# A convolution and feed-forward kernel: step 1's blocks cross the partition halves on ScalarE instead of by SyncE's transfers

## The chip, the cores and the metric

The kernel runs on one core of one Trainium2 chip. The metric is the device time of one launch in microseconds: 2280.98 us as the median of three timed runs (2280.73 to 2281.51). One more run was taken with the hardware profiler; all rows shown are from it. TensorE (PE) multiplies, VectorE (DVE), ScalarE (ACT) and GpSimd (POOL) compute elementwise, SyncE (SP) issues transfers, and POOL issues transfers too. All transfers are carried out by the same 16 DMA engines.

## The reference

A causal convolution of width 7 along the sequence, with one softmax-normalized filter for each of 8 heads, followed by a feed-forward block with a quick GELU:

```python
batch, seq, d_model = (8, 4096, 192)      # kernel_size 7, n_heads 8
w = np.exp(w - max); w = w / (sum + 1e-09)
out = np.einsum('hk,bskhg->bshg', w, x_unf)          # the convolution
h = x @ w_in                                         # [32768, 192] @ [192, 2048]
g = h * (1.0 / (1.0 + np.exp(-1.702 * h)))
return (g @ w_out).astype(np.float32)                # [32768, 2048] @ [2048, 192]
```

The weights arrive as 64-bit floats and are turned into 32-bit ones on the chip.

## The kernel before

The 32768 tokens are worked off in 32 steps ("big" 0 to 31) of two batches with 512 tokens each. A step has two products. The first one (line 614) multiplies the convolved input by w_in, the second one (line 989, in step 0 lines 820 and 825) multiplies the activated result by w_out. From step 1 on both are written in a Strassen-like form with fewer multiplications: sums of input blocks, of weight blocks ("forms") and of result blocks take the place of some matmuls. The schedule is written out by hand; each engine works through its own instructions in program order.

The tile `conv_t` has 3 planes of 13 blocks, each 128 partitions by 256 columns. `own(big)` is plane 0 for even steps and plane 2 for odd ones; plane 1 is shared. The convolution writes six blocks (C11 to C32) into the step's own plane, and `sums_c` adds seven or eight more (V1 to V8). The product works on pairs of partition halves, so every block is also needed with its halves exchanged: upper 64 partitions to the lower 64 and the other way round, in plane 1. `cross(big, b0, b1)` makes that copy with two transfers on SyncE's queue (line 541).

- `prepare(big)` lists the convolution's VectorE work, the sums and the crossings. In step 1 the sums run on VectorE, in later steps on POOL (line 393 and 391). Its first crossing is that of V1 alone, which opens the step: `fetch` multiplies with it first. Then blocks C11 to C22 cross, and at the end of the list all others.
- `cross_when` holds a crossing back until the plane is free; for step 1 the two larger ones are therefore issued together, in the middle of step 0's second product, where `need("all 1")` stands. In later steps the crossings are cut into pieces of three blocks (`pieces`), spread over the second product.
- Step 0's second product is `second_first`. While it runs, `add_forms` makes the forms: copies on ScalarE (line 435 and 433) and additions done by accumulating transfers which POOL issues (line 437). ScalarE also copies partial results there: `act.copy(to, dst)` (line 827), c12 and c21 from bank `a` (lines 864 and 873), and the sums of line 885.
- In the same stretch the taps of step 2's convolution begin: `tap` multiplies on ScalarE (line 516). The taps of one third are then added up by accumulating transfers, issued by POOL in `end_taps` (line 530), and those of another third by POOL itself (line 518). V1 of step 2 needs both.
- `end_forms` (line 441) turns the signs of four forms on ScalarE during step 1's first product, `hidden`, after their accumulating transfers have landed. ScalarE's copies of line 651, activations of lines 636 and 640 and VectorE's sums of line 655 belong to `hidden` too. In step 1, the transposes of the next input (line 473, `turn_next`) and one sum (`EARLY_G_1`) stand in the second half of `hidden` on VectorE; in later steps the transposes stand in the first half, and that sum is an accumulating transfer.

The order on POOL's queue in this stretch is: accumulations of the forms (line 437), three accumulations of taps (g<-g, line 530), one more into `conv_t`, the last four accumulations of the forms, two more of taps, then the six adds of line 518 and the sums of line 393 and 391, the first of which is V1 of step 2.

Of the kernel before, what the change touches and what calls it, by code (L numbers as in the profile page):

```python
# [15 lines left out]
def kernel(  # L16
# [29 lines left out]
    nc = tc.nc  # L46
# [34 lines left out]
    vec, act = nc.vector, nc.scalar  # L81
    halves = [slice(0, R), slice(R, P)]
# [75 lines left out]
    conv_t = consts.tile([P, 3, NB, T], F32)  # L158
# [17 lines left out]
    def own(big):  # L176
        return conv_t[:, big % 2 * 2, :, :]
# [135 lines left out]
    for c in range(NC):  # L313
        part = sel[:, c, :].rearrange("i (h q) -> i h q", h=2)
        for sign in (1, -1):
            nc.gpsimd.affine_select(
                out=part,
                in_=part,
# [219 lines left out]

    def cross(big, b0, b1):
        for o in range(2):  # L540
            nc.sync.dma_start(
                out=conv_t[halves[1 - o], 1, b0:b1, :], in_=own(big)[halves[o], b0:b1, :]
            )

    def copy_over(b):

# [9 lines left out]
    def cross_now(early, big, b0, b1):  # L556
        if early or big == 1:
            cross(big, b0, b1)
        else:
            pieces.extend((big, b, min(b + 3, b1)) for b in range(b0, b1, 3))  # L560

    def cross_piece():
        if pieces:
            cross(*pieces.pop(0))
# [729 lines left out]
```

## Time and profile before

| | us |
|---|---|
| median of three timed runs | 2280.98 |
| lowest, highest | 2280.73, 2281.51 |
| profiled execution, its own time | 2281.64 |
| its span, first to last instruction | 2279.60 |
| DVE busy in the span | 1942.0 |
| ACT busy | 1563.4 |
| POOL busy | 849.1 |

How to read the rows: in a timeline row stand the start in us, the duration in us, the engine, the source line, the operation, the names written and read, shapes and how many instructions were merged; in brackets the idle time of the engine before it and what ended it. In a row of stretches stand from:to, the length, then for each engine its busy time and its number of instructions, then the granted TensorE clock as a share of full speed, the share of the DMA engines and GB/s; where only one line is asked for, PE and PEld (weight loads) alone stand there. In the chain of waits: start, duration, what. In the DMA view: the queue's packets, MB and share of the 16 engines, or an issue's names, count, KB each and the median us from issue to landing. In groups by line: count, busy us, mean ns of one, idle time before.

### The profile page before, as it was taken

Reading aid. Unit: us, or ns where it says so; the run is one execution under the profiler, and the core shown is the slowest. Engines: PE = TensorE matmul, PEld = TensorE weight load, DVE = VectorE, ACT = ScalarE, POOL = GpSimd, SP = SyncE. Lnnn points to the kernel's source line nnn. Section 1 sums busy time; section 2 is a strip of 40 time slices with the busy share of each in tenths; the row PEclk is TensorE's granted clock in tenths of the full one; section 3 lists DMA queues with packets and bytes.
Section 4 is the critical chain, followed back from the end, with each engine's and each line's share of the span. In section 5 each row is a group of like instructions: output and inputs, shape, how many; then the busy total and the mean of one; then the engine's idle time right before and its main releaser. Section 6 shows DMA issues by size and latency. Waiting matters only on the chain.

```text
span 2279.6 us, 60958 instructions
## 1 busy us (share of the span) xinstructions
PE 2268.2 (100%) x25214; PEld 1198.7 (53%) x25214; DVE 1942.0 (85%) x2794; ACT 1563.4 (69%) x2968; POOL 849.1 (37%) x834
## 2 busy tenths in 40 slices
PE   9999999999999999999999999999999999999999
PEld 5445555555555555555555555555555555555556
DVE  8888888888888888888888888888888888888877
ACT  8657766677766677666776666776667766667754
POOL 1544442344432444424444233443244442344400
PEclk9999999999999999999999999999999999999999
DMA  9976566665567565666656666556756566674443
GB/s 205 161 147 136 117 118 126 130 136 114 113 126 144 121 132 113 128 127 126 139 114 117 126 134 132 121 111 125 142 120 135 114 127 128 124 142 83 91 99 70
DMA packets 270227, 285.76 MB, mean 125 GB/s; under 512 B 118016, under 2 KB 206080, under 8 KB 269824
## 3 DMA queue, kind: packets, MB, share of 16 engines
q0 software_dynamic: 57648, 150.69, 36.8%
q1 hardware_dynamic: 210656, 130.80, 25.5%
q8 instruction: 198, 3.24, 0.6%
q14 instruction: 77, 0.63, 0.1%
q10 hardware_dynamic: 1648, 0.39, 0.1%
HBM read 53.15 MB, written 25.17 MB: 34 GB/s over the span
## 4 chain that ended last, share of the span: by engine, by line
PE 98%; DMA 1%; ACT 0%; DVE 0%; POOL 0%; issue 0%; SPq 0%; DVEq 0%; ACTq 0%; POOLq 0%
PE slot L614 35%; PE slot L989 34%; PE sums L614 15%; PE sums L989 12%; PE slot L820 2%; DMA w_out_s<-w_form 1%; DMA xin<-in_x_dram 0%; POOL conv_t L518 0%; ACT conv_t L1094 0%; DVE xt L473 0%; DMA conv_t<-conv_t 0%; DVE conv_t L504 0%; SPq L99 0%; ACT conv_t L357 0%; ACT conv_t L356 0%
## 5 line engine op out<-in xcount | busy, mean ns | idle before, releaser
L614 PE MATMUL slot<-conv_t,w_in_s 64*128 64x512 f32 x3740 | 864.9, 592 | 4.5 <-DMA conv_t<-conv_t 2.6
L989 PE MATMUL slot<-g,w_form 128*32 128x256 f32 x7024 | 710.4, 379 | 0.0
L614 PEld LDWEIGHTS slot<-conv_t,w_in_s 64*128 64x128 f32 x3740 | 373.2, 187 | 435.3 <-issue 356.8
L393 DVE TENSOR_TENSOR g<-g 128x1024 f32<-128x1024 f32 x372 | 449.1, 1235 | 4.5 <-ACT g L640 1.3
L989 PEld LDWEIGHTS slot<-g,w_form 128*32 128x32 f32 x7024 | 372.9, 110 | 120.4
L614 PE MATMUL sums<-conv_t,w_in_s 64*128 64x512 f32 x1660 | 409.4, 591 | 0.3 <-DVE w_in_s L376 0.3
L640 ACT ACTIVATE g<-room 128x1024 f32<-128x1024 f32 x310 | 325.8, 1077 | 72.1 <-DVE room L655 70.2
L1014 ACT COPY room<-slot 32x256 f32<-32x256 f32 x434 | 159.3, 367 | 310.9 <-PE slot L989 309.8
L989 PE MATMUL sums<-g,w_form 128*32 128x256 f32 x2648 | 368.8, 379 | 0.0
L989 PE MATMUL slot<-g,w_out_s 128*32 128x256 f32 x4080 | 318.9, 380 | 0.0
L965 POOL DMA_DIRECT2D g<-g x124 | 106.2, 857 | 496.2 <-PE slot L989 157.7
L614 PEld LDWEIGHTS sums<-conv_t,w_in_s 64*128 64x128 f32 x1660 | 171.4, 187 | 186.9 <-issue 140.8
L518 POOL TENSOR_TENSOR conv_t<-conv_t,g 128x512 f32<-128x512 f32 x180 | 261.6, 1453 | 14.1 <-POOL conv_t L518 2.6
L530 POOL DMA_DIRECT2D g<-g x120 | 104.7, 890 | 421.3 <-PE sums L989 128.7
L651 ACT COPY room<-slot 128x512 f32<-128x512 f32 x434 | 231.5, 601 | 40.3 <-PE slot L614 40.3
L516 ACT ACTIVATE g<-xt,cw 128x512 f32<-128x512 f32 x360 | 248.7, 730 | 2.2
L989 PEld LDWEIGHTS slot<-g,w_out_s 128*32 128x32 f32 x4080 | 164.5, 110 | 132.9 <-ACT g L636 22.7
L636 ACT ACTIVATE g<-slot 128x512 f32<-128x512 f32 x334 | 180.8, 598 | 45.1 <-PE slot L614 24.6
L989 PEld LDWEIGHTS sums<-g,w_form 128*32 128x32 f32 x2648 | 177.8, 110 | 36.8
L504 DVE SCALAR_TENSOR_TENSOR conv_t<-xt,cw,conv_t 128x512 f32<-128x512 f32 (+1 forms) x198 | 190.7, 963 | 4.6
L393 POOL TENSOR_TENSOR conv_t<-conv_t 128x256 f32<-128x256 f32 x180 | 186.8, 1051 | 9.4
L1014 ACT COPY room<-sums 32x256 f32<-32x256 f32 x217 | 79.6, 367 | 144.2 <-PE sums L989 142.5
(204 smaller groups left out, 2903.9 us busy)
## 6 DMA issues: line engine op xcount, KB each, us to landing
g<-g POOLq DMA_DIRECT2D x124, 512.0 KB, 5.7
xin<-in_x_dram SPq DMA_DIRECT2D x240, 180.0 KB, 4.3
conv_t<-conv_t SPq DMA_DIRECT2D x180, 192.0 KB, 3.2
g<-g POOLq DMA_DIRECT2D x120, 256.0 KB, 3.7
out_dram<-osbs SPq DMA_DIRECT2D x186, 128.0 KB, 5.0
g<-room POOLq DMA_DIRECT2D x31, 512.0 KB, 5.5
conv_t<-g POOLq DMA_DIRECT2D x60, 256.0 KB, 4.7
g<-osbs POOLq DMA_DIRECT2D x30, 512.0 KB, 4.7
```

What stands on the lines that cost most here:

```text
L393: eng.tensor_sub(v(dst), v(a), v(b))
L504: vec.scalar_tensor_tensor(out=dst, in0=src, scalar=tap, in1=dst, op0=ALU.mult, op1=ALU.add)
L516: act.mul(home, conv_src(big, c, k), cw[:, c, k : k + 1])
L518: nc.gpsimd.tensor_add(dst, dst, home)
L530: nc.gpsimd.dma_start(out=out, in_=src, accum_op=ALU.add)
L614: nc.tensor.matmul(slot[h], w_in_s[halves[h], a, v * P : (v + 1) * P], src, start=first, stop=True, skip_group_check=True,)
L636: act.activation(dst[:, :, h, :], src[h].rearrange("p (o t) -> p o t", o=2), AF.Gelu_apprx_sigmoid)
L640: act.activation(dst.rearrange("p o h t -> p h o t"), src.rearrange("p h (o t) -> p h o t", o=2), AF.Gelu_apprx_sigmoid,)
L651: act.copy(bank(dst, h), bank(src, h))
L965: nc.gpsimd.dma_start(out=spot(dst), in_=spot(a), accum_op=ALU.add)
L989: nc.tensor.matmul(dst, w, t, start=first, stop=last, skip_group_check=True)
L1014: act.copy(to, d)
```

## The change

The copies that `cross` makes for step 1 go from SyncE's transfers to copies by ScalarE, except where only one block is copied (V1, the one that opens the step). That is two calls with two halves each: blocks C11 to C22 (64 partitions by 1024) and the eight blocks from C31 on (64 by 2048). All other steps keep their transfers.

```diff
     def cross(big, b0, b1):
         for o in range(2):
-            nc.sync.dma_start(
-                out=conv_t[halves[1 - o], 1, b0:b1, :], in_=own(big)[halves[o], b0:b1, :]
-            )
+            out, src = conv_t[halves[1 - o], 1, b0:b1, :], own(big)[halves[o], b0:b1, :]
+            if big == 1 and b1 - b0 > 1:
+                act.copy(out, src)
+            else:
+                nc.sync.dma_start(out=out, in_=src)
```

On ScalarE the four copies stand, in program order, between the fourth copy of line 827 (room<-slot, 76.60 us in the profile) and the fifth (81.75 us); on SyncE the four transfers stood behind the pair for V1 and ahead of step 0's stores. The order of instructions on PE, VectorE and POOL is the same as before.

## The prediction

> **What bounds the kernel now.** First the head of the profile's page: TensorE (PE) is busy for 2268.2 of 2279.6 us, so any gain has to come out of some 11 us in which PE waits, or out of time in which it runs slowly.
>
> ```profile
> span 2279.6 us, 60958 instructions
> ...
> PE 2268.2 (100%) x25214; PEld 1198.7 (53%) x25214; DVE 1942.0 (85%) x2794; ACT 1563.4 (69%) x2968; POOL 849.1 (37%) x834
> ```
>
> Then the stretches, for the matmuls of line 614 alone: the first product of step 1, beside that of step 3, which has the same 168 matmuls.
>
> ```profile
> 93.11:139.44 46.33, 42.15 (x168) 23.87 (x168) 0.93 0.76 136
> 383.52:419.77 36.25, 36.25 (x168) 16.70 (x168) 1.00 0.57 112
> ```
>
> Step 1 takes 10.1 us more, at a mean granted clock of 0.93. PE's timeline and the stretches with all engines say where:
>
> ```profile
> 117.96 1.18 PE L614 MATMUL slot<-conv_t,w_in_s 64*128 64x512 f32 x3 [1.56 <-ACT room L651]
> 135.03 4.47 PE L614 MATMUL slot<-conv_t,w_in_s 64*128 64x512 f32 x12 [2.61 <-DMA conv_t<-conv_t]
> ```
> ```profile
> 119.20:122.60 3.40, 3.40 (x10) 1.79 (x8) 3.40 (x3) 2.17 (x4) 2.82 (x3) 0.50 1.04 194
> 136.30:139.70 3.40, 3.40 (x12) 1.36 (x12) 0.83 (x2) 0.00 (x0) 3.10 (x4) 0.50 1.12 223
> ```
>
> Two stalls, 1.56 and 2.61 us, and after each 3.4 us at half clock, which cost 1.7 us of work each: 7.6 us. Smaller slips make up the other 2.5.
>
> The rule that speaks against counting the clock: the Trainium skill, TensorE: Matmul & The Clock Gate, section "HAM oscillation — how this bites in real kernels", asks for "no PE-idle gaps >~3.4µs". Both idle times here are shorter, and each is followed by 0.50; I go by the rows, and the rule's own result is a rival below.
>
> Third the chain of waits: what is late before each stall?
>
> ```profile
> 105.10 11.73 DMA w_out_s<-w_form
> ...
> 116.91 0.52 ACT w_form L441
> 117.43 0.48 ACT room L651
> ...
> 131.63 0.74 POOL conv_t L393
> ...
> 132.90 2.00 DMA conv_t<-conv_t
> ```
>
> Stall 1 is ScalarE (ACT), held by an accumulating transfer that POOL issued at 105.1. Stall 2 is step 2's opening block V1, summed on POOL at 131.63 and only then sent across. Both lead to POOL's queue, whose timeline is:
>
> ```profile
> 94.66 1.85 POOL L437 DMA_DIRECT2D w_form<-w_form  x2 [13.07 <-DMA w_form<-w_form]
> 96.20 3.98 POOL L530 DMA_DIRECT2D g<-g  x3
> 102.73 1.19 POOL L530 DMA_DIRECT2D conv_t<-g  x1 [2.55 <-PE slot L614]
> ...
> 108.18 1.20 POOL L530 DMA_DIRECT2D g<-g  x1 [0.69 <-DMA g<-g]
> 119.70 1.19 POOL L530 DMA_DIRECT2D conv_t<-g  x1 [10.32 <-DMA g<-g]
> 120.45 11.10 POOL L518 TENSOR_TENSOR conv_t<-conv_t,g 128x512 f32<-128x512 f32 x6
> ```
>
> POOL stands 13.07 us until 94.66 for one landing, and everything behind it, including the six adds that end in V1, is pushed back. (The 2.55 us put down to PE are more likely the landing of the first g<-g, which this transfer reads.) What are the transfers stuck behind? The DMA view from 79 to 93 us, and the first row of the same view from 63 to 75:
>
> ```profile
> q0 software_dynamic: 930, 1.26, 54.8%
> q1 hardware_dynamic: 310, 1.53, 48.8%
> ...
> w_form<-w_form POOLq DMA_DIRECT2D x2, 192.0 KB, 14.7
> ```
> ```profile
> q0 software_dynamic: 1348, 2.12, 110.7%
> ```
>
> The 16 engines are full. From 79 to 93 POOL's transfers (software queue) share them with SyncE's (hardware queue), and these are the transfers that the change removes.
>
> **The change, part by part.** It removes four transfers, two of 256 KB and two of 512 KB (1.57 MB). Step 1's V1 pair and all later steps stay.
>
> Removed from DMA: 48.8% of 14 us is 6.8 us of all 16 engines. The other way: alone, POOL's queue moved 2.12 MB in 12 us, 0.177 MB/us; its 1.26 MB would take 7.1 us and end near 86 instead of 93. So POOL's 94.66 becomes about 87.7.
>
> The Trainium skill, SBUF — State Buffer, "SBUF: two separate sides", warns of another cause: POOL cannot write its descriptors while VectorE holds the port they share. By that rule the 13 us would stay, which is the "no change" rival; full engines speak against it.
>
> Added to ACT: four copies of 64 partitions, 1024, 1024, 2048 and 2048 wide, between L827 at 76.60 and L827 at 81.75.
>
> ```profile
> 76.60 0.58 ACT L827 COPY room<-slot 32x512 f32<-32x512 f32 x1 [1.17 <-PE slot L825]
> 81.75 0.58 ACT L827 COPY room<-sums 32x512 f32<-32x512 f32 x1 [4.57 <-PE sums L825]
> 83.51 0.56 ACT L873 COPY slot<-slot 96x512 f32<-96x512 f32 x1 [1.18 <-PE slot L820]
> 85.60 0.73 ACT L516 ACTIVATE conv_t<-xt,cw 128x512 f32<-128x512 f32 x1 [1.52 <-DVE xt L473]
> ...
> 91.08 1.95 ACT L516 ACTIVATE g<-xt,cw 128x512 f32<-128x512 f32 x3
> ...
> 110.50 1.06 ACT L640 ACTIVATE g<-room 128x1024 f32<-128x1024 f32 x1 [1.61 <-DMA conv_t<-g]
> ...
> 116.91 0.52 ACT L441 ACTIVATE w_form<-w_form 128x384 f32<-128x384 f32 x1 [1.19 <-DMA w_out_s<-w_form]
> ```
> ```profile
> L548 ACT COPY conv_t<-conv_t 64x256 f32<-64x256 f32 x4 | 1.6, 404 | 0.5 <-DVE conv_t L504 0.4
> L640 ACT ACTIVATE g<-room 128x1024 f32<-128x1024 f32 x5 | 5.3, 1094 | 1.6 <-DMA conv_t<-g 1.6
> ```
> ```profile
> 78.25 1.62 DVE L393 TENSOR_TENSOR conv_t<-conv_t 128x256 f32<-128x256 f32 x4
> ```
> ```profile
> 86.11 0.63 PE L820 MATMUL slot<-osbs,w_out_s 128*32 128x512 f32 x3
> ```
>
> A half-to-half copy of 256 takes 0.40; an activation of 1024 takes 1.09, so each element adds (1.09 - 0.40)/768 = 0.9 ns and a copy of 2048 takes 2.0. Bounds: 1.9 if the fixed part overlaps, 3.2 if it grows as the 256 copy does (8 x 0.40). I take 2.0, nearest to the wide row. The narrow pair runs from 77.2 to 79.4. The wide pair waits for VectorE's last sum, which ends at 79.87, and ends at 83.9. Queued behind are L827 (ends 84.5 instead of 82.3), L873 (85.1 instead of 84.1), then L516 at 85.60, which waited for VectorE anyway. PE needs L873's bank at 86.11. So it costs nothing: 4.57 + 1.18 + 1.52 us of ACT idleness hide it, with 1.0 us to spare; at the upper bound (1.6 and 3.2 us a copy) L873 ends at 87.9 and PE loses 1.8. A gain from the blocks arriving sooner is excluded: PE starts on them at 93.11 without a wait.
>
> What follows on POOL: the three g<-g need ScalarE's taps (L516), the last of which ends at 93.03. With an issue of 1.19 the group ends about 94.2 instead of 100.18, 6 us sooner. conv_t<-g follows its first landing, so it and the issue at 105.10 come 6 to 8 us sooner; with the same 11.73 us of flight w_out_s<-w_form lands by 111, before ACT asks at about 114. ACT recovers the 1.19 before 116.91 and the 1.61 before 110.50, 2.8 together, more than the 1.56 that PE stalled. Stall 1 goes with its clock window: 3.3 us.
>
> For stall 2, the issue at 108.18 waits for the third g<-g. It comes 5 us sooner if flights stay long, and 11 if they shrink towards the 3.7 us of the page's row for the whole run:
>
> ```profile
> g<-g POOLq DMA_DIRECT2D x120, 256.0 KB, 3.7
> ```
>
> I take 9, as the engines are then nearly empty until 97. V1 lands at 134.9 - 9 = 126, and PE, 3.8 us sooner itself (3.3 and about 0.5 of slips), asks at 132.4 - 3.8 = 128.6. Stall 2 goes as well: 2.6 + 1.7 = 4.3 us. At 5 us sooner 1.3 us of it would be left.
>
> What is late next: VectorE at the end of step 1. Its rows of step 1 (first three, with the page's mean) and of step 3:
>
> ```profile
> 120.13 3.15 DVE L393 TENSOR_TENSOR osbs<-g 128x1024 f32<-128x1024 f32 x1
> ...
> 128.98 2.08 DVE L473 STREAM_TRANSPOSE xt<-xin 128x576 f32<-128x576 f32 x3
> ```
> ```profile
> L393 DVE TENSOR_TENSOR g<-g 128x1024 f32<-128x1024 f32 x372 | 449.1, 1235 | 4.5 <-ACT g L640 1.3
> ```
> ```profile
> 415.65 1.28 DVE L655 TENSOR_TENSOR room<-room,slot 128x512 f32<-128x512 f32 x2 [1.54 <-PE slot L614]
> ...
> 419.87 1.28 DVE L655 TENSOR_TENSOR room<-room,slot 128x512 f32<-128x512 f32 x2 [0.60 <-PE slot L614]
> ```
>
> In its second half step 1 has the transposes (2.08) and one add (1.24) that step 3 has elsewhere: 3.3 us against 2.14 us of idleness in step 3. VectorE ends 1.2 us late, and the second product needs it at once. Before, stall 2 covered that. I charge 1.0 (from 0, if PE has some slack, to 3.1, if one L393 again takes 3.15 instead of 1.24 beside POOL's adds).
>
> Sum: 7.6 (stalls and windows) + 1.2 (half of the 2.5 of slips; 0 to 2.5) - 1.0 = 7.8 us. The profiled run took 2281.64 us around its span of 2279.6, 0.66 above the median of the three timed; off both comes the same 7.8, so 2273.8 for that run and **2273.2** as a median.
>
> **The rivals.** (A) Stall 2 stays: only the first part of POOL's chain moves, V1 still waits for flights that collide with out_dram and xin loads. Gain 3.3 + 0.5, 2277.2. For: the flights after 97 us are as loaded as before. (B) VectorE's tail is longer: a stall of 1.6 brings its own 1.7 of half clock, 3.3 instead of 1.0, 2275.5, and up to 3.1 + 1.7, 2277.0. For: the 3.15 row. Against: POOL's adds move ahead of that stretch. (C) No change, 2281.0: POOL waits for descriptors, not for engines. Against: 54.8% and 48.8% fill them. (D) Slower: ACT becomes the bound before 93 us. If copies across halves of this width run at half the rate, the wide pair takes 8 us, ends at 87.9, and L873 at 89.1: PE waits 3.0 and loses 1.7 to the clock, and the taps, 3.5 us later, end at 96.5, where POOL issues today, so nothing is recovered: 2285.7. It begins to decide when a wide copy takes over 2.5 us (79.9 + 5.0 + 1.15 = 86.1). Against: L548 does the same move without such a penalty. (E) The clock windows come by themselves and stay, so the stalls alone go, 4.2 us: 2276.8. Against: nowhere else before the end does a window stand without a stall. That is what the page on the clock gate would give.
>
> **How the numbers follow.** Forecast 0.68, A 0.06, B 0.13, C 0.06, D 0.05, E 0.02. A measurement of this kernel can tell about 0.2%, 4.6 us, from no change, so faster means under 2276.4: forecast and two thirds of B, 0.77. Same: the rest of B, A, C and E, 0.18. Slower: D, 0.05. The range begins at 2270.9 (all 10.1 us recovered) and ends at 2277.2, which takes in B and A and leaves out C and D.
>
> **What would show it.** Right: POOL's L437 starts near 88 instead of 94.66; the 1.56 and 2.61 us of PE idleness and both stretches at 0.50 are gone; the first product of step 1 takes 37 to 39 us; four ACT copies end near 84, and PE starts at 86.1 as before. Wrong: L437 still near 94 (C); PE late at 86.1 (D); a wait on conv_t<-conv_t near 128 (A); a wait on VectorE or a 0.50 stretch at the start of the second product (B).

## The result, and the profile after

The changed kernel takes 2273.79 us as the median of seven runs (2273.21 to 2274.41), against 2280.98 (2280.08 to 2282.35) for the kernel before: a ratio of 0.9968, with a 95% interval of 0.9957 to 0.9980. The forecast was 2273.2 in a range of 2270.9 to 2277.2.

| | before | forecast | after |
|---|---|---|---|
| POOL's L437 behind its long wait starts | 94.66 | near 88 | 86.70 |
| V1 of step 2 has landed | 134.90 | 126 | 125.94 |
| first product of step 1, us | 46.33 | 37 to 39 | 37.43 |
| second product of step 1, us | 33.91 | 34.9 | 34.81 |
| PE's last matmul starts | 2274.20 | | 2266.26 |
| median, us | 2280.98 | 2273.2 | 2273.79 |

(Lines behind the edit have moved by two: L614 is now L616, L655 is L657, L989 is L991. The copies are L543, V1's transfers L545.) The head of the page, after:

```profile
span 2272.6 us, 60950 instructions
...
PE 2263.4 (100%) x25214; PEld 1214.9 (53%) x25214; DVE 1941.0 (85%) x2794; ACT 1568.8 (69%) x2972; POOL 847.0 (37%) x834
```

PE's busy time fell by 4.8 us although it runs the same 25214 matmuls: one at half clock counts as busy for longer (with the traffic put back, below, one of the same line takes 1.19 us at half clock and 0.59 at full). The rest of the gain was idleness. The stretches of step 1's two products, one view for the matmuls of each line; columns are stretch, length, PE and weight loads, clock, DMA share, GB/s:

```profile
93.00:130.43 37.43, 37.43 (x168) 25.22 (x168) 1.00 0.76 137
```
```profile
130.43:165.24 34.81, 34.42 (x624) 30.14 (x624) 1.00 0.84 169
```

The mean clock of the first product went from 0.93 to 1.00, and PE is busy through all of it. The second product is 0.9 us longer than before (33.91), and the view of PE's waits between 80 and 165 us holds one line only:

```profile
PE slot L991 <- DVE room L657: 0.4, 1, 0.4
```

That is the wait on VectorE's tail for which the prediction had charged 1.0; as a wait it is 0.4 of the 0.9 us, and 0.75 went when the tail was made shorter (below). Where the first product's gain comes from is seen on POOL's timeline, next to the rows shown of before:

```profile
86.70 0.86 POOL L437 DMA_DIRECT2D w_form<-w_form  x1 [5.95 <-DMA w_form<-w_form]
87.77 0.86 POOL L437 DMA_DIRECT2D w_form<-w_form  x1 [0.21 <-DVE w_in_s L391]
...
91.98 2.42 POOL L530 DMA_DIRECT2D g<-g  x2 [0.55 <-ACT g L516]
94.69 1.19 POOL L530 DMA_DIRECT2D conv_t<-g  x1 [0.29 <-issue]
...
96.52 2.93 POOL L437 DMA_DIRECT2D w_out_s<-w_form  x2
98.23 2.45 POOL L530 DMA_DIRECT2D g<-g  x1
109.85 1.19 POOL L530 DMA_DIRECT2D conv_t<-g  x1 [9.17 <-DMA g<-g]
110.60 11.98 POOL L518 TENSOR_TENSOR conv_t<-conv_t,g 128x512 f32<-128x512 f32 x6
```

The wait of 13.07 us shrank to 5.95. What stood behind it came sooner by 8.0 us (L437), 9.95 (the g<-g at 98.23 instead of 108.18) and 9.85 (the adds at 110.60 instead of 120.45). At the end of this chain stand V1's two transfers, on SyncE's timeline and in the DMA view from 123 to 125:

```profile
123.43 1.11 SPq L545 DMA_DIRECT2D conv_t<-conv_t  x2
```
```profile
conv_t<-conv_t SPq DMA_DIRECT2D x2, 64.0 KB, 1.9
```

The second is issued at 123.99 and lands at 125.94. The DMA view from 79 to 93 us:

```profile
q0 software_dynamic: 1392, 1.83, 82.2%
...
w_form<-w_form POOLq DMA_DIRECT2D x4, 192.0 KB, 5.2
```

The hardware queue, 48.8% before, is gone from this stretch; POOL's queue moves 1.83 MB instead of 1.26, and the median of its w_form landings is 5.2 us (four of them) instead of 14.7 (two). The price, on ScalarE's timeline:

```profile
76.98 2.09 ACT L543 COPY conv_t<-conv_t 64x1024 f32<-64x1024 f32 x2
79.78 3.83 ACT L543 COPY conv_t<-conv_t 64x2048 f32<-64x2048 f32 x2 [0.70 <-issue]
83.52 0.57 ACT L829 COPY room<-sums 32x512 f32<-32x512 f32 x1
84.11 0.56 ACT L875 COPY slot<-slot 96x512 f32<-96x512 f32 x1
85.42 0.72 ACT L516 ACTIVATE conv_t<-xt,cw 128x512 f32<-128x512 f32 x1 [0.75 <-DVE xt L473]
```

Four copies in 5.9 us, and L516 still finds its data last at 85.42. PE's waits show nothing near 86.

### The profile page after: what moved, and what is told of

It reads as the page before. It is cut to its first block, busy times and chain, and to the rows that moved or that the text cites. A ratio compares the mean times of both kernels' runs of the same rounds, so it can differ in the third digit from the quotient of the medians.

```text
span 2272.6 us, 60950 instructions
## 1 busy us (share of the span) xinstructions
PE 2263.4 (100%) x25214; PEld 1214.9 (53%) x25214; DVE 1941.0 (85%) x2794; ACT 1568.8 (69%) x2972; POOL 847.0 (37%) x834
## 4 chain that ended last, share of the span: by engine, by line
PE 99%; DVE 1%; ACT 0%; DMA 0%; issue 0%; SPq 0%; ACTq 0%; DVEq 0%
PE slot L616 35%; PE slot L991 33%; PE sums L616 16%; PE sums L991 13%; PE slot L822 2%; DMA xin<-in_x_dram 0%; DVE room L657 0%; DVE xt L473 0%; ACT conv_t L1096 0%; DVE conv_t L504 0%; SPq L99 0%; ACT conv_t L357 0%; DVE room L393 0%; ACT conv_t L356 0%; DVE g L391 0%
## 5 line engine op out<-in xcount | busy, mean ns | idle before, releaser
L616 PE MATMUL slot<-conv_t,w_in_s 64*128 64x512 f32 x3740 | 862.5, 591 | 0.3 <-DVE w_in_s L376 0.3
L991 PE MATMUL slot<-g,w_form 128*32 128x256 f32 x7024 | 710.8, 379 | 0.4 <-DVE room L657 0.4
L616 PEld LDWEIGHTS slot<-conv_t,w_in_s 64*128 64x128 f32 x3740 | 377.6, 187 | 423.9 <-issue 347.7
L393 DVE TENSOR_TENSOR g<-g 128x1024 f32<-128x1024 f32 x372 | 448.9, 1234 | 3.2
L991 PEld LDWEIGHTS slot<-g,w_form 128*32 128x32 f32 x7024 | 375.7, 110 | 118.1 <-DVE room L657 0.9
L616 PE MATMUL sums<-conv_t,w_in_s 64*128 64x512 f32 x1660 | 408.3, 589 | 0.3 <-DVE w_in_s L376 0.3
L991 PE MATMUL sums<-g,w_form 128*32 128x256 f32 x2648 | 368.8, 379 | 0.0
L991 PE MATMUL slot<-g,w_out_s 128*32 128x256 f32 x4080 | 318.8, 380 | 0.0
L616 PEld LDWEIGHTS sums<-conv_t,w_in_s 64*128 64x128 f32 x1660 | 172.1, 187 | 184.9 <-issue 140.0
L518 POOL TENSOR_TENSOR conv_t<-conv_t,g 128x512 f32<-128x512 f32 x180 | 262.2, 1457 | 16.3 <-POOL conv_t L518 3.0
L653 ACT COPY room<-slot 128x512 f32<-128x512 f32 x434 | 231.4, 601 | 38.5 <-PE slot L616 38.4
L516 ACT ACTIVATE g<-xt,cw 128x512 f32<-128x512 f32 x360 | 248.5, 730 | 2.2
L991 PEld LDWEIGHTS slot<-g,w_out_s 128*32 128x32 f32 x4080 | 164.7, 110 | 128.5 <-ACT g L638 22.7
L991 PEld LDWEIGHTS sums<-g,w_form 128*32 128x32 f32 x2648 | 177.9, 110 | 37.6
L504 DVE SCALAR_TENSOR_TENSOR conv_t<-xt,cw,conv_t 128x512 f32<-128x512 f32 (+1 forms) x198 | 192.0, 970 | 4.6
L393 POOL TENSOR_TENSOR conv_t<-conv_t 128x256 f32<-128x256 f32 x180 | 181.9, 1024 | 9.4
```

The lines of the kernel that those rows point to most:

```text
L393: eng.tensor_sub(v(dst), v(a), v(b))
L504: vec.scalar_tensor_tensor(out=dst, in0=src, scalar=tap, in1=dst, op0=ALU.mult, op1=ALU.add)
L516: act.mul(home, conv_src(big, c, k), cw[:, c, k : k + 1])
L518: nc.gpsimd.tensor_add(dst, dst, home)
L616: nc.tensor.matmul(slot[h], w_in_s[halves[h], a, v * P : (v + 1) * P], src, start=first, stop=True, skip_group_check=True,)
L653: act.copy(bank(dst, h), bank(src, h))
```

## The experiments

**The traffic put back.** The copies stay on ScalarE, and four transfers of the same sizes run beside them. They write extra data into parts of the output that later steps overwrite, so work is added.

```diff
                 act.copy(out, src)
+                at = ((4 * o + 3) * S + S - 2 * TOK) * D + (0 if b0 == 0 else R * 4 * T)
+                nc.sync.dma_start(out=flat_out[at : at + R * (b1 - b0) * T].rearrange("(p n) -> p n", p=R), in_=src)
```

> The changed kernel, and beside its four copies on ScalarE four transfers of the same sizes on SyncE's queue at the same place, from the same blocks into rows of the output that step 31 overwrites later (DRAM in place of the other partition half); nothing waits for them. Theory (the removed transfers' share of the 16 engines held POOL's accumulating transfers back): POOL's L437 that now starts at 86.7 us goes back to 92 to 95, both stalls of TensorE in step 1 and their half-clock stretches return, 2279.5 to 2281.5 us. Rival (what helped is that the blocks reach the other half sooner, or that SyncE's queue is shorter): the blocks still arrive by ScalarE at 84 us, so it stays within 1 us of 2273.8.

Measured: 2280.38 us (eleven runs, 2277.99 to 2282.11) against 2281.0 for before beside it, ratio 0.9997 [0.9988, 1.0006]. The DMA view from 79 to 93 us, then POOL's and PE's timelines of this kernel (its lines have moved by four more, so L620 is L616):

```profile
q0 software_dynamic: 931, 1.26, 55.2%
q1 hardware_dynamic: 294, 1.47, 44.1%
```
```profile
94.02 0.86 POOL L437 DMA_DIRECT2D w_form<-w_form  x1 [12.64 <-DMA w_form<-w_form]
```
```profile
116.22 1.18 PE L620 MATMUL slot<-conv_t,w_in_s 64*128 64x512 f32 x3 [0.58 <-ACT room L657]
...
133.01 3.02 PE L620 MATMUL slot<-conv_t,w_in_s 64*128 64x512 f32 x6 [3.56 <-DVE g L391]
```

With the traffic the gain is gone and POOL waits 12.64 us again, while ScalarE, VectorE and the copies are those of the changed kernel. So it is the transfers that held POOL, not who does the copy. That they did it by filling the engines is read from the views (55.2% and 44.1% here, 82.2% for POOL's queue alone). The loss is spread otherwise than before: stall 1 is only 0.58, stall 2 is 3.56.

**One pair alone.** In two kernels only the narrow pair (four blocks wide) or only the wide pair (eight) goes to ScalarE.

```diff
-            if big == 1 and b1 - b0 > 1:
+            if big == 1 and b1 - b0 == 4:
```

> Only the pair of 1024 columns (blocks C11 to C22, 0.52 of the 1.57 MB) goes to ScalarE, the wide pair stays on SyncE. Theory (engine time, in proportion to bytes): a third of the 8 to 9 us by which POOL's chain moved, so L437 at about 92, step 2's V1 lands about 132; stall 1 goes, stall 2 grows to over 4 us because TensorE comes sooner, net 1.5 to 3.5 us under before: 2277.5 to 2279.5. Rival (the wide pair's long rows are what crowds POOL's queue out): no gain here, 2280 to 2281.

> Only the pair of 2048 columns (1.05 of 1.57 MB) goes to ScalarE, the narrow pair stays on SyncE. Theory (in proportion to bytes): two thirds of the shift, L437 at about 89.5, V1 lands about 128.9, 1.7 us after TensorE asks for it, and a half-clock stretch follows: 2275.5 to 2277.5. Rival (the wide pair alone crowds POOL's queue out): the whole gain, 2273.3 to 2274.3, no stall above 1 us in step 1.

Measured: the narrow pair alone 2279.36 (ten runs, 2276.99 to 2280.88), ratio 0.9990 [0.9981, 0.9999]; the wide pair alone (== 8 in the same line) 2274.27 (six runs, 2273.47 to 2276.87), ratio 0.9972 [0.9961, 0.9983]. The narrow pair fell where a gain in proportion to bytes has it, the wide pair did not: it brings nearly everything. POOL's rows (the first is of the narrow pair alone, the second of the wide) show that the proportion holds roughly where the transfers act:

```profile
92.25 1.86 POOL L437 DMA_DIRECT2D w_form<-w_form  x2 [12.08 <-DMA w_form<-w_form]
```
```profile
88.82 0.86 POOL L437 DMA_DIRECT2D w_form<-w_form  x1 [8.09 <-DMA w_form<-w_form]
```

POOL goes on 2.4 us sooner than before with a third of the bytes gone (94.66 to 92.25), 5.8 with two thirds, and 8.0 with all (exact thirds of 8.0 would be 2.7 and 5.3). What PE makes of that is decided at V1: its second transfer lands, and PE's next matmul starts, at these times of the trace.

| | V1 landed | PE's next matmul | PE could have started it |
|---|---|---|---|
| before | 134.90 | 135.03 | 131.84 |
| traffic put back | 132.88 | 133.01 | 128.87 |
| narrow pair alone | 131.35 | 131.48 | 127.35 |
| wide pair alone | 127.49 | 127.62 | 127.24 |
| after | 125.94 | 127.28 | 127.28 |

In the first four PE starts 0.13 us behind the landing, whoever is named as releaser (VectorE's L391, in the rows here): V1 is what PE waits for. In the last PE isn't held. (The third column is the start less the time that the gap in front of this matmul is longer than that in front of the same one in step 3.) PE's stall with the narrow pair alone, and the stretch behind it with all engines:

```profile
131.48 4.44 PE L616 MATMUL slot<-conv_t,w_in_s 64*128 64x512 f32 x11 [3.54 <-DVE g L391]
```
```profile
132.52:135.93 3.41, 3.41 (x10) 1.71 (x6) 0.61 (x1) 0.00 (x0) 3.28 (x4) 0.50 1.16 231
```

The narrow pair alone removes stall 1, so PE reaches V1 4.5 us sooner; V1 comes only 3.55 sooner, and stall 2 grows from 2.61 to 3.54. The wide pair alone brings V1 7.4 us sooner, and PE loses 0.38 on it; of the last 1.55 us that the narrow pair adds, PE can use these 0.38, and the rest is slack.

**ScalarE made slower.** One, then both of the wide copies are made twice; the repeats change no value.

```diff
                 act.copy(out, src)
+                if b1 - b0 == 8 and o == 1:
+                    act.copy(out, src)
```

> The changed kernel with one of ScalarE's two wide copies done twice, so that ScalarE is busy about 1.9 us longer. Theory (four copies cost nothing because ScalarE idled there, with about 1 us to spare): L875, which ended at 84.7, ends at about 86.6, TensorE waits 0.5 to 0.8 us near 86 and keeps its full clock: 2274.2 to 2275.0. Rival (ScalarE has ample room): 2273.8 within 0.4.

> Both wide copies done twice, about 3.8 us more on ScalarE. Theory: L875 ends at about 88.4, TensorE waits about 2.5 us near 86, and a stretch of 3.4 us at half clock follows, 1.7 us more: 2277 to 2279. Rival on the clock (half clock only after 3.4 us of idleness): 2276 to 2276.8, clock 1.00 throughout.

Measured: one more copy 2274.2 (five runs, 2273.59 to 2274.5), ratio 0.9965 [0.9952, 0.9978]; two more 2276.95 (ten runs, 2275.71 to 2278.03), ratio 0.9978 [0.9969, 0.9987]. PE's timeline of the first, then of the second, with the stretch behind the second's stall (L877 is the L875 of the changed kernel):

```profile
86.52 0.63 PE L824 MATMUL slot<-osbs,w_out_s 128*32 128x512 f32 x3 [0.54 <-ACT slot L877]
```
```profile
88.10 1.06 PE L824 MATMUL slot<-osbs,w_out_s 128*32 128x512 f32 x3 [2.12 <-ACT slot L877]
```
```profile
88.16:91.57 3.41, 3.41 (x20) 0.84 (x24) 3.31 (x9) 1.25 (x2) 0.00 (x0) 0.50 0.58 91
```

A copy of 1.90 us costs 0.54 of stall, so the slack in front of PE is 1.4. Two cost 2.12 (2.4 less the 0.36 us by which the wide copies began sooner in that execution, at 79.30 against 79.66) and the half clock behind it, and the first product then starts at 96.80 instead of 93.00: 3.8 = 2.1 + 1.7. That prices the window by itself, at a place where the kernel has no other stall. The first product itself is as long as before (37.36): V1's issues move from 123.43 to 126.94, by 3.5 us, and PE by 3.8.

**VectorE's tail made shorter.** Two of step 1's sums on g, which end its first product, are put into the second product; in a second kernel the copies and transposes at the end of step 0 are in another order as well.

```diff
-    EARLY_G_1 = EARLY_G[:2] + [EARLY_G[2][:1], [(8, 8, "+", 0)] + EARLY_G[3]]
+    EARLY_G_1 = EARLY_G[:2] + [EARLY_G[2][:1], []]
+    LATE_G_1 = {("sum", 14, 14, "-", 18): (8, 8, "+", 0), ("sum", 8, 8, "-", 16): (2, 9, "-", 0)}
...
+            if big == 1 and item in LATE_G_1:
+                sum_g(*LATE_G_1[item])
```

The second kernel moves these lines too:

```diff
-        turn(0, 0, blocks(p1), js)
-        turn(1, 1, blocks(p5), js)
         add(q12, q12, whole(c12))
         turn(1, 0, blocks(whole(c21)), js)
+        turn(0, 0, blocks(p1), js)
         store(0, 0)
+        turn(1, 1, blocks(p5), js)
```

> The changed kernel with the two sums that step 1 makes on VectorE just before the last result sum of its first product moved into the second product (behind its first and its fourth sum). Theory (VectorE is late at the end of step 1 by what it does more there, and TensorE loses about 1.0 us to it): the wait of 0.39 us on VectorE's L657 and the excess of 1.0 us at the start of step 1's second product go, 2272.7 to 2273.3. Rival (TensorE is held there by something else, or VectorE's delay only moves on): 2273.6 or more.

> As the one before, and the end of step 0 on VectorE in another order: the sum that reads bank c12 and the transposition that reads bank c21 come ahead of the two that read SBUF, as TensorE waits for those banks at about 96.5 us (0.58 us lost against step 3 in both kernels). Theory: that 0.58 us goes as well: 2272.0 to 2272.8. Rival (another wait takes its place): as the one before.

Measured: 2274.22 (2273.37 to 2274.48), ratio 0.9966 [0.9954, 0.9979], and 2274.52 (2274.13 to 2275.32), 0.9969 [0.9956, 0.9981], five runs each: no gain. The second products of the two:

```profile
130.35:164.41 34.06, 34.02 (x624) 20.06 (x624) 1.00 0.84 171
```
```profile
130.29:164.33 34.04, 34.01 (x624) 20.06 (x624) 1.00 0.84 168
```

PE did gain the 0.75 us there, and the time didn't show it. Of the 0.58 us at 96.5 nothing was won: the first product takes 37.35 and 37.36 us in the two (37.43 in the changed kernel), and in the second of them the same matmul, `sums` at 96.86, is put down to a wait on ScalarE's L653 (0.23). The rival, another wait in its place, was right there. Then the second of these kernels was run again beside the changed kernel itself on one chip, together with one in which the tail is made longer by a sum that is made twice:

```diff
+    EARLY_G_1 = EARLY_G[:2] + [EARLY_G[2][:1], [(8, 8, "+", 0)] + EARLY_G[3] * 2]
```

> The kernel after, with one of VectorE's last adds of step 1's first product (1.2 us) made twice in place; the output is the same. Theory of this run (rival B's price): VectorE's tail at the start of the second product grows by 1.2, so the stall at the first room sum grows from 0.4 to about 1.6 us; a stall of that size is followed by a stretch at half clock of 3.4 us, which costs 1.7 more. The second product takes 34.8 + 1.2 + 1.7 = 37.7 us, and the median is some 2.9 us above the kernel after: near 2276.7. Other theory: the half clock comes only from stalls of 2 us or more (the shortest that were followed by it were 1.56 with another small wait beside it, and 2.1), so the stall alone is paid: 36.0 us and 2275.0. Third: the tail is not on PE's path, and nothing changes: 34.8 us and 2273.8.

> The kernel after as it is, on the same chip and against the same runs of before as the two beside it. Expected: 2273.8 us, or up to 0.5 above it on a chip whose runs of before are slower than 2281.

> The kernel after with two of VectorE's sums moved from step 1's first product into its second, and the copies and transposes at the end of step 0 in another order; nothing is left out. Theory (the 1.0 us charged for VectorE's tail is real time): PE ends 0.8 to 0.9 us sooner than in the kernel after, and the median is 0.8 us lower than that of the kernel after beside it. Other theory (what PE gains at 133 us, the last stores take back): the medians agree within 0.2 us.

Measured, before beside them at 2281.59: longer tail 2275.28 (nine runs, 2274.82 to 2275.97), ratio 0.9974 [0.9964, 0.9984]; the changed kernel 2273.92 (six runs, 2272.95 to 2274.07), 0.9967 [0.9955, 0.9979]; shorter tail 2273.93 (six runs, 2273.82 to 2274.75), 0.9970 [0.9958, 0.9981]. PE's stall and second product with the longer tail:

```profile
134.12 1.70 PE L991 MATMUL slot<-g,w_form 128*32 128x256 f32 x25 [1.44 <-DVE room L657]
```
```profile
130.32:166.18 35.86, 34.42 (x624) 29.67 (x624) 1.00 0.81 163
```

A longer tail is paid: 1.05 us more of second product, 1.36 more of time (2275.28 - 2273.92), with every run above every run of the changed kernel. The clock stayed at 1.00, as the second theory had it. A shorter tail gains nothing that shows; in this execution of it the second product took 34.34, a gain of 0.47, and the runs of one kernel lie about 1 us apart. Whether a few tenths are gained stays open.

## Why the prediction was right

**What was removed.** The rate at which POOL's queue had drained alone, 0.177 MB/us from 63 to 75 us, put L437 at 87.7; it came at 86.70. The rival "no change", in which POOL waits for VectorE's port, fell twice over. VectorE is busy for 13.76 of the 14 us from 79 to 93, before and after alike, and yet POOL's wait is halved; and the wait is back as soon as the transfers alone are:

```profile
79.00:93.00 14.00, 14.00 (x125) 3.84 (x116) 13.76 (x25) 11.12 (x15) 5.58 (x6) 1.00 0.83 133
```

(Stretch, length, then PE, weight loads, VectorE, ScalarE and POOL.)

**What was added.** 2.0 us for a wide copy was measured as 1.92, the narrow pair at 2.09 in all against 2.2. L875 ends at 84.67 where 85.1 was forecast, and the slack is 1.4 instead of 1.0. The point from which ScalarE would decide was put at 2.5 us for a wide copy; by this slack it is 2.6. What the slower rival got wrong lies behind that point: it had the taps' delay give the whole gain back. With ScalarE 3.8 us slower the kernel is still 4.8 us faster than before beside it, where the changed one is 7.2 faster: it loses 2.4 (3.2 by the two medians alone, which were not taken side by side) and keeps the rest. PE, late itself by 3.8, asks for V1 later too.

**The chain on POOL.** The group of g<-g ends at 94.4 (forecast 94.2), the second w_out_s<-w_form is issued at 97.27 and lands at 106.37 (by 111), and the transfer behind the third g<-g comes 9.95 us sooner. Of the two bounds, 5 and 11, the choice of 9 was the step with the most riding on it, and V1 landed at 125.94 for a forecast of 126. That it fell so close is in part luck: the issue behind the third g<-g came 9.95 us sooner, and POOL's six adds then took 11.98 us instead of 11.10. The mechanism was half as described. The third g<-g was in flight for 4.46 us instead of 9.97, as the empty engines had it; the one issued at 98.23 took 11.33, as long as before (11.23), as the rival that keeps stall 2 had it. The margin was thinner than the text had it. It let PE ask at 128.6, counted from the modelled end of the matmul before; PE's start was at 127.28. Of the difference 0.6 us is that matmul's length, and 0.7 are slips that were gained too and not taken off this time. With 0.13 from landing to start, 1.2 us were left. At the 5 us bound V1 would have landed at 129.9 and PE would have lost 2.7 us and probably a clock window, where the text left 1.3: the rival that keeps stall 2 was nearer than its chance.

**The sum.** Stalls and windows 7.6, slips 1.2: together 8.8 in the first product, measured 46.33 - 37.43 = 8.9. VectorE's tail 1.0: measured 34.81 - 33.91 = 0.9. Total 7.8; PE's last matmul starts 7.94 us sooner. The rows of the kernel before, and after:

```profile
2274.20 0.38 PE L989 MATMUL sums<-g,w_form 128*32 128x256 f32 x1
```
```profile
2266.26 0.38 PE L991 MATMUL sums<-g,w_form 128*32 128x256 f32 x1
```

**The 0.6 us of the miss.** The median moved by 7.2, not 7.8, and the span by 7.0. In the second comparison of the same two kernels it moved by 7.7 (2281.59 to 2273.92), so the miss is about what two comparisons differ by. One part of such a difference shows at the end of the kernel. Behind PE's last matmul come ScalarE's last copy and the stores that it issues itself; after, the copy waits for three such issues:

```profile
2265.01 2.39 ACTq L919 DMA_DIRECT2D out_dram<-osbs  x3
2267.44 0.36 ACT L1016 COPY room<-sums 32x256 f32<-32x256 f32 x1 [2.12 <-DMA out_dram<-osbs]
```

In the second profile of the very same kernel the three issues take 1.36 us, and the span is 2272.0 instead of 2272.6. So the kernel's end varies by some tenths from one execution to the next, and the prediction, which had carried the end over unchanged, has no term for it.

**The clock.** That the windows go with their stalls (against the rival that keeps them, and gives 2276.8) is shown by the first product at 1.00, and the other way round by the stall of 2.12 that brought a window to 88 us. The price of the rival with a longer tail was half wrong: 1.44 us of idleness brought no window.

## What to carry to other kernels

A transfer that nobody waits for can still cost time by what it takes from the transfers beside it: look at which queue's landings stretch while the engines are full, and follow what its issuer has standing behind them. Gains in such a chain arrive in proportion to the bytes at the place itself, and as thresholds at the end: here 2.4 us at POOL were worth 1.6, 5.8 were worth 6.7, and 8.0 no more than 7.2. A stall of 2 us in front of TensorE cost its clock 1.7 more, so what takes it away altogether is worth more than what shortens it.

## What the runs showed of the hardware that was not expected

Where the half clock begins: idle times of 0.54, 0.58 and 1.44 us were followed by none, and 1.56, 2.12, 2.61 and 3.54 by one stretch of 3.41 us each. After 3.56 us of idleness, in the kernel with the traffic put back, two stretches follow on each other. When the clock changes says why. In all twelve traces every change of the granted clock stands a whole number of 3.413 us behind its first rise: before, the rise is at 6.58 us and the changes at 119.22, 122.64, 136.29 and 139.71 are 33, 34, 38 and 39 such cells later. So idleness has to be counted by cells. Three cells of the kernel with the traffic put back, then two of the narrow pair alone (length, PE's busy time, ..., clock):

```profile
129.02:132.43 3.41, 0.43 (x2) 0.00 (x0) 3.41 (x6) 2.43 (x5) 3.17 (x5) 1.00 0.15 36
132.43:135.84 3.41, 2.83 (x8) 1.68 (x10) 2.24 (x2) 0.78 (x1) 3.25 (x3) 0.50 0.92 224
135.84:139.26 3.42, 3.42 (x16) 1.18 (x16) 0.76 (x2) 0.00 (x0) 1.58 (x3) 0.50 1.10 229
```
```profile
125.69:129.10 3.41, 2.25 (x11) 0.81 (x7) 3.41 (x6) 1.85 (x3) 3.17 (x4) 1.00 0.00 0
129.10:132.52 3.42, 1.04 (x5) 0.89 (x7) 3.42 (x4) 2.56 (x4) 3.26 (x4) 1.00 0.53 141
```

The 3.56 us lie 2.98 in one cell and 0.58 in the next, which is at half clock already, and the half clock stays for one cell more; the 3.54 lie 1.2 and 2.4, and only the second brings a stretch. From the first rise to PE's last matmul, the twelve traces have five cells with more than 1.44 us of idleness (1.56, 2.12, 2.16, 2.37, 2.98); each of them is followed by 0.50, and no other cell at full clock is. So what a stall costs in clock also hangs on how it lies in the cells; a stall of 2 us halved by a boundary would cost none by this count, which no run here shows.

The Trainium skill, TensorE: Matmul & The Clock Gate, section "HAM oscillation — how this bites in real kernels", asks for no idle gap above some 3.4 us. Every idle time here but the last two is well below that, and three of them are followed by 0.50, so in these runs the limit lies between 1.44 and 1.56 us in one cell, if it is idle time alone that sets it (the one of 1.44 stands in the second product, whose matmuls are shorter).

VectorE's taps ran into POOL's adds once these came sooner. Before, then after:

```profile
110.12 1.53 DVE L504 SCALAR_TENSOR_TENSOR conv_t<-xt,cw,conv_t 128x512 f32<-128x512 f32 x2
```
```profile
110.02 4.56 DVE L504 SCALAR_TENSOR_TENSOR conv_t<-xt,cw,conv_t 128x512 f32<-128x512 f32 x2
```

```profile
L518 POOL TENSOR_TENSOR conv_t<-conv_t,g 128x512 f32<-128x512 f32 x180 | 262.2, 1457 | 16.3 <-POOL conv_t L518 3.0
```

Together the two took 3.0 us longer: 2.88 us instead of 0.74 for the first, 1.65 instead of 0.75 for the second, and each ended 0.56 us behind one of POOL's adds (110.60 for 1.74 us, 112.42 for 1.61; the mean of all is 1457 ns). By the Trainium skill, SBUF — State Buffer, "SBUF: two separate sides", an operation of VectorE with two operands in SBUF and one of GpSimd that reads SBUF shut each other out for a whole instruction, and the one that starts first goes first. The rows agree with the shutting out, not with the order: the first L504 is recorded from 110.02 on, 0.58 us ahead of the add that it waited for. Spans on POOL are rough, so this stays open. PE didn't wait for these taps, so here it cost nothing: the L393 that took 3.15 us before is down to 1.21, and other operations of VectorE wait instead.
